# Ten instead of eight token blocks by Strassen products, with copies on ScalarE and the softmax division on GpSimd

## The chip, the cores and the metric

The kernel runs on one core of a Trainium2 chip. The metric is the device time of one execution in microseconds (us), taken as the median of three runs. Beside it there is one profiled execution, which leaves a trace of every instruction.

## The reference

There are 8 batches of 8 heads, 576 positions and head size 64. The attention keeps only the scores within tau of the row's maximum; its result, heads side by side, feeds a layer with an exact gelu (4608 tokens, 512 wide, 2048 hidden).

```python
scores = scale * np.matmul(q, k.transpose(0, 1, 3, 2))
thresh = np.max(scores, axis=-1, keepdims=True) - tau
scores = np.where(scores >= thresh, scores, -1000000000.0)
scores = scores - np.max(scores, axis=-1, keepdims=True)
attn = np.exp(scores)
attn = attn / (np.sum(attn, axis=-1, keepdims=True) + 1e-09)
x = (attn @ v), as (B, H, S, D) -> (B*S, H*D)
h = x @ w_in
g = 0.5 * h * (1.0 + erf(h / sqrt(2)))
out = g @ w_out
```

The two weight matrices come as 64-bit floats; the kernel makes 32-bit floats of them from their bits.

## The kernel before

**Work and its pieces.** Two heads make a pair, and there are 32 pairs, four to a batch. A pair's scores are made in chunks of 128 query rows: for each of the first four chunks both heads side by side, and in a fifth, small one the last 64 rows of both heads together. One such chunk step is a slot (`scores`, `softmax_head`, `softmax_tail`), so a pair has five slots, and a batch 20. In a slot TensorE writes scores into two PSUM tiles of two banks each (tag `sc`, two buffers; the fifth slot uses one); VectorE takes each row's negated maximum (L368); GpSimd makes the threshold from it (L369); ScalarE takes the exponential (L371); VectorE then compares the scores with the threshold and multiplies (L387, with a row sum), which frees the score tile for the next slot. VectorE turns the result in 32x32 blocks (L434, L432), and SyncE's DMAs put these together as pT (`regroup`, L456 and L452). Two slots into the next pair, TensorE multiplies v by pT (`weigh_v`, L473, in two parts of 320 and 256 tokens), and the result, x transposed, is divided by the row sums on its way from PSUM to the x tiles (L490, VectorE). The reciprocals travel through DRAM and come back on all partitions as inv (`divisors`, L409 to L422).

**The first batch is done in another way.** Its four pairs (the "early" ones, slots 0 to 19: first chunks 0 and 1 of all four pairs, then the rest of each) are transposed by TensorE with a diagonal matrix of reciprocals (`turn_p_early`, L302), copied from PSUM by ScalarE (L310, L320) and, for the last chunk, by VectorE (L313, L325). Meanwhile the weights are converted in 32 pieces: `conversions` takes exponents (L178, VectorE), rebases them (L179, ScalarE), takes mantissas (L185) and puts these together (L187, L189). This needs three tiles of the pool `gp` for each piece, which also holds the gelus' results.

**The MLP.** The 4608 tokens are 18 blocks of 256. Ten are plain: `block_steps` yields the products one by one, 64 of the first layer (hT, L530, 256 columns) and 32 of the second (o_ps, L543, 512 columns), and `fill` puts as many into each slot, behind its scores, as a written plan allows. On TensorE a product of 32-bit floats is two instructions in the trace. The plan is GOAL: so many blocks done by such a slot, with PARTS sharing a pair's amount among its five slots (1.2, 1.2, 0.8, 1.2, 0.6). Every engine takes its instructions in the order written. A gelu (L509) needs another table of ScalarE's than the exponentials do, so each row of gelus is followed by a tiny exponential that brings the other table back (`table`, L516): two table loads per row. From slot 20 on, the gelus that have come due are done after the next slot's exponentials; in the early slots on even slots only, and as they come.

**The last stage.** The other eight blocks are done two at a time after all attention (`strassen`, L663), by the seven products of quarters that Strassen's scheme, in Winograd's form, needs in place of eight. The tokens are one dimension of a quarter: the two blocks of a pair are its two halves. The x of blocks that wait for this stage stays in the pool `xg` (seven tiles), but three of them (AWAY: blocks 10 to 12) are written to DRAM as soon as they are ready (`put_away`, SyncE) and fetched back during the stage (`bring`).

**GpSimd** also issues the DMAs of later pairs' q, k and v (`load_steps`, one step a slot: q in slot 1, k in slot 2, v in slots 3 and 4, four DMAs each). Queries are multiplied by the scale on ScalarE (L338) in slot 2, between VectorE's transposes of k and q (L337, L339).

Of the kernel before, what the change touches and what calls it, by code (L numbers as in the profile page):

```python
# [8 lines left out]
FP32 = mybir.dt.float32  # L9
U32 = mybir.dt.uint32  # L10
U8 = mybir.dt.uint8
AF = mybir.ActivationFunctionType
# [6 lines left out]
def kernel(  # L19
# [33 lines left out]
    P = 128  # L53
# [11 lines left out]
    N_DF = d_ff // P  # L65
    TOK = 256
    N_BLK = B * S // TOK
    PLAIN = N_BLK - 8

    AWAY = [PLAIN, PLAIN + 1, PLAIN + 2]  # L70
    order = list(range(PLAIN + 3, N_BLK)) + AWAY
    DUOS = list(zip(order[0::2], order[1::2]))
    assert 2 * D == P and 2 * TAIL == P and HALF <= 512 and N_DM == HP and B * S % TOK == 0 and S % Q == 0 and TOK == 2 * P
    SLOTS = NC + 1
# [86 lines left out]
    def conversions():  # L161

        vec = nc.vector
        ahead = None  # L170
        while raws or ahead:
            piece = None
            if raws:
                dst, raw, shifted = raws.pop(0)
                hi = raw.rearrange("p (f w) -> p f w", w=2)[:, :, 1]
                top = shifted.rearrange("p (f w) -> p f w", w=2)[:, :, 0]
                expo, power = (gp.tile([P, PIECE], U32, tag="g", name=s) for s in ("expo", "power"))
                vec.tensor_scalar(expo, hi, 0x7FF00000, None, op0=ALU.bitwise_and)  # L178
                nc.scalar.activation(power, expo, AF.Relu, bias=rebias, scale=8.0)  # L179
                piece = dst, hi, top, power  # L180
                yield 340
            if ahead:
                dst, hi, top, power = ahead
                mant = gp.tile([P, PIECE], U32, tag="g", name="mant")
                vec.tensor_scalar(mant, top, 0x0FFFFFFF, 0x10000000, op0=ALU.bitwise_and, op1=ALU.bitwise_or)  # L185
                yield 340
                vec.scalar_tensor_tensor(power, hi, 0x80000000, power, op0=ALU.bitwise_and, op1=ALU.bitwise_or)  # L187
                yield 720
                vec.scalar_tensor_tensor(dst, mant, 2.0 ** -28, power.bitcast(FP32), op0=ALU.mult, op1=ALU.mult)  # L189
                load_piece()  # L190
                converted[0] += 1
                yield 700
            ahead = piece
# [98 lines left out]
    def turn_p_early(p, i):  # L292


        s = st[p]
        if i == 0 or (p < HP and i == 2):
            s["pT"] = [one.tile([P, KR, S], FP32, tag=f"pT{e}", name=f"pT{e}") for e in range(2)]
        w, diag = s.pop(("p", i)), s.pop(("diag", i))
        n = 1 if i == NC else 2

        def turn(to, cols, e):
            nc.tensor.matmul(to, lhsT=w[:, cols], rhs=diag[:, e, :], start=True, stop=True)  # L302

        for e in range(n):
            tr = ps.tile([P, NC, P], FP32, tag="mm", name="tr")
            for c in range(NC):
                at = e * (S + TAIL) + c * P
                turn(tr[:, c, :], slice(at, at + P), e)
            if i < NC:
                nc.scalar.copy(s["pT"][e][:, 0:NC, i * P:(i + 1) * P], tr)  # L310
        if i == NC:
            for e in range(2):
                nc.vector.tensor_copy(s["pT"][e][:, 0:NC, MAIN:S], tr[:, :, e * TAIL:(e + 1) * TAIL])  # L313
        tails = s["pT"][0][:, NC, :]
        tr = ps.tile([P, NC, P], FP32, tag="mm", name="tr")
        if i < NC:
            for e in range(2):
                at = MAIN + e * TAIL
                turn(tr[e * TAIL:(e + 1) * TAIL, 0, :], slice(at, at + TAIL), e)
            nc.scalar.copy(tails[:, i * P:(i + 1) * P], tr[:, 0, :])  # L320
            return
        turn(tr[0:TAIL, 0, :], slice(MAIN, S), 0)
        for e in range(2):
            rows = slice(e * TAIL, (e + 1) * TAIL)
            nc.vector.tensor_copy(tails[rows, MAIN:S], tr[0:TAIL, 0, rows])  # L325

    def turn_qk(p):

        s = st[p]
        qT = s["qT"] = ld.tile([P, MAIN], FP32, tag="qT", name="qT")
        kT = s["kT"] = ld.tile([P, S], FP32, tag="kT", name="kT")
        qt = s["q_tail"] = q_tail[p % 4]
        qs, ks = s.pop("q"), s.pop("k")
        nc.vector.transpose(kT.rearrange("p (b i) -> p b i", i=Q), ks)  # L337
        nc.scalar.activation(qs, qs, AF.Copy, bias=0.0, scale=q_scale)  # L338
        nc.vector.transpose(  # L339
            qT.rearrange("p (c a i) -> p c a i", c=NC, i=Q),  # L340
            qs[:, 0:MAIN // Q, :].rearrange("p (a c) j -> p c a j", c=NC))
        for e in range(2):
            rows = slice(e * D, (e + 1) * D)
            nc.vector.transpose(
                qt[rows, e * TAIL:(e + 1) * TAIL].rearrange("p (b i) -> p b i", i=Q), qs[rows, MAIN // Q:NB, :])
# [112 lines left out]
    def weigh_v(p, lo, hi):  # L458
# [5 lines left out]
        for c in range(KR):  # L464
            for e in range(2):
# [4 lines left out]
                else:  # L470
# [1 line left out]
                    rhs = by_64(s["pT"][e])[:, lo // (2 * Q):hi // (2 * Q), c, :]  # L472
                nc.tensor.matmul(  # L473
                    to, lhsT=s["v"][:, e, c, :], rhs=rhs, start=(c == 0), stop=(c == KR - 1))
        by = None if p < EARLY else s["inv"]
        if hi == S:
            del st[p]

        def divide():
            at = lo  # L480
            while at < hi:
                n, o = divmod(b * S + at, TOK)
                size = min(TOK - o, hi - at)
                if n not in x_blk:
                    x_blk[n] = xg.tile([P, N_DM, TOK], FP32, tag="x", name="x")
                to, x = x_blk[n][:, hp, o:o + size], xT[:, at - lo:at - lo + size]
                if by is None:
                    nc.scalar.copy(to, x)
                else:
                    nc.vector.tensor_tensor(to, x, by[:, at:at + size], op=ALU.mult)  # L490
                at += size

        if by is not None:
            return divide
        divide()


    NS_IN, NS_OUT = 4 * TOK / 2.4, 4 * d_model / 2.4
# [2 lines left out]
    late = []  # L501
    lag = [1]
    dirty = [False]
    def gelus(left):

        while len(late) > left:
            g, j, hT = late.pop(0)
            t = gp.tile([P, 2, TOK], FP32, tag="g", name="g")
            nc.scalar.activation(t, hT, AF.Gelu)  # L509
            g[j - 1], g[j] = t[:, 0, :], t[:, 1, :]  # L510
            dirty[0] = True

    def table():

# [4 lines left out]
    def block_steps(n):  # L519
# [15 lines left out]
        for m in range(TOK // P):  # L535
            for j in range(N_DF):
                mlp["layer"] = 2
                yield NS_OUT, len(pieces) - N_DF + j + 1
                if j not in g:
                    gelus(0)  # L540
                if j == 0:
                    o = ps.tile([P, 512], FP32, tag="mm", name="o_ps")
                nc.tensor.matmul(o[:, 0:d_model], lhsT=g[j][:, m * P:(m + 1) * P], rhs=w_out_sb[j],  # L543
                                 start=(j == 0), stop=(j == N_DF - 1))
# [237 lines left out]
    BATCH = HP * SLOTS  # L782
    WIDE = 5 * 2 * Q
    WEIGH = 2
    START = 2 * HP + 2

    GOAL = [(-1, 0.0), (START - 1, 0.0), (BATCH - 1, 0.55)]
    GOAL += [(BATCH * (m + 2) + WEIGH, x) for m, x in enumerate([1.96, 3.3, 4.64, 5.98, 7.32, 8.66, PLAIN])]

    def goal(n):  # L790
        for (lo, x), (hi, y) in zip(GOAL, GOAL[1:]):
# [7 lines left out]
    tokens = 0  # L799
    owed = 0.0  # L800
    due = []
    loads = iter(())
    for n in range(len(slots) + WEIGH + 1):
        p, i = slots[n] if n < len(slots) else divmod(n, SLOTS)
# [4 lines left out]
            softmax_head(p, i)  # L809
        elif n == len(slots):  # L810
            ext = weights_in()
        if not early or n % 2 == 0:
            gelus(0)
            table()
        made = []
        for args in due:
            weigh_v(*args)
        due = []
        if p > EARLY and i == WEIGH:
            made = [weigh_v(p - 1, lo, hi) for lo, hi in ((0, WIDE), (WIDE, S))]  # L820
        owed += (goal(n) - goal(n - 1)) * BLK_NS * (PARTS[i] if not early and p < NP else 1.0)
        if early:
            fill(owed, tokens)
# [3 lines left out]
            turn_p_early(*last)  # L827
        if p < NP:
            softmax_tail(p, i)
        if made:  # L830
            made[0]()
        if p < NP and not early:
            turn_p(p, i)
        if made:
            made[1]()
        if p < NP and not early:
            if i == 2:
                regroup(p, 1)
# [16 lines left out]
        if n == BATCH:  # L855
            for t in pd_tail + [turned_p[:, e, h, :, :] for e in range(2) for h in range(2)]:
                nc.gpsimd.memset(t[:, NB:4 * KR, :], 0.0)
        if p >= HP and i == 1 and p + 2 < NP:
            loads = load_steps(p + 2)
        if p >= HP:  # L860
            next(loads, None)
        if p >= HP - 1 and i == 2 and p + 1 < NP:
            turn_qk(p + 1)
        convert(3000 if n < 2 * HP else 3650 if n < BATCH - 1 else 1e9)
# [11 lines left out]
        if n == START - 1:  # L876
            tokens = TOK
        elif n == BATCH + 1:
            tokens = S
        elif p > EARLY and i == WEIGH and p % HP == 0:  # L880
            tokens = p // HP * S
            for n in AWAY:
                if n in x_blk and (n + 1) * TOK <= tokens:
                    put_away(n)
    fill(1e12, B * S)
    strassen(*ext)

# [31 lines left out]
```

## Time and profile before

| what | us |
|---|---|
| median of 3 runs (1420.29 to 1422.51) | 1420.45 |
| profiled execution, its own time | 1423.59 |
| its span in the trace | 1421.8 |
| TensorE matmuls busy | 1382.1 (97%) |
| VectorE busy | 892.6 (63%) |
| ScalarE busy | 640.9 (45%) |
| GpSimd busy | 388.0 (27%) |
| table loads on ScalarE, 71 ahead of gelus and 71 behind | 91.1 each |
| division on VectorE (L490), 104 instructions | 31.8 |
| first Strassen product starts | 1028.79 |

Three stages follow each other. To about 160 us the first batch and the weights are prepared; to about 1029 us come 28 pairs of attention, with plain blocks between their steps; then four passes of two blocks by Strassen. In the page's slices each digit is one fortieth of the span, 35.5 us, in tenths of busy time. In the chain and the timeline a line gives start, duration, engine, line and operation, and in brackets how long an engine was idle before, and on whom it waited.

### The profile page before, as it was taken

What the parts mean: (1) busy time and instruction counts of PE and PEld (TensorE: products, weight loads), DVE (VectorE), ACT (ScalarE), POOL (GpSimd) and SP (SyncE); (2) the same over time, 40 slices, a digit from 0 to 9 for tenths busy, and PEclk for the clock granted to TensorE, in tenths of its full rate; (3) what the DMA queues carried; (4) which work ended last, traced back from release to release, by engine and by line L of the source; (5) the groups of instructions that cost most, each with busy time, mean ns of one, the idle gap of its engine ahead of it and who ended that gap; (6) DMA issues with size and microseconds to landing.
All of it is one profiled execution on the core that took longest, in us unless ns stands there. A gap on an engine that the chain in (4) does not pass through costs nothing.

```text
span 1421.8 us, 19662 instructions
## 1 busy us (share of the span) xinstructions
PE 1382.1 (97%) x6544; PEld 958.8 (67%) x6544; DVE 892.6 (63%) x1788; ACT 640.9 (45%) x1040; POOL 388.0 (27%) x812
## 2 busy tenths in 40 slices
PE   6898999999999999999999999999999999999999
PEld 4666547566466574665756647566588888888887
DVE  5887777777777777777777777777764142241330
ACT  5758525436356273462645727547141140230320
POOL 4443244434433433434434434430000000000000
PEclk9999999999999999999999999999999999999999
DMA  9977167776666676666766666674500000001000
GB/s 265 295 264 243 38 145 150 148 156 129 134 136 148 146 156 129 146 135 149 162 148 146 158 146 150 141 160 101 106 3 8 23 1 26 19 1 48 12 8 23
DMA packets 219347, 167.05 MB, mean 117 GB/s; under 512 B 122480, under 2 KB 203952, under 8 KB 219248
## 3 DMA queue, kind: packets, MB, share of 16 engines
q1 hardware_dynamic: 193040, 108.65, 36.2%
q0 software_dynamic: 23808, 56.57, 13.1%
q8 instruction: 53, 0.87, 0.3%
q10 hardware_dynamic: 2400, 0.59, 0.2%
q14 instruction: 46, 0.38, 0.1%
HBM read 71.68 MB, written 11.47 MB: 58 GB/s over the span
## 4 chain that ended last, share of the span: by engine, by line
PE 87%; DVE 5%; ACT 5%; DMA 2%; issue 1%; SPq 0%; POOL 0%; DVEq 0%; ACTq 0%; POOLq 0%
PE bank L663 27%; PE o_ps L543 18%; PE hT L530 18%; PE sc L356 12%; PE xT L473 10%; ACT p L371 1%; DVE p L387 1%; PE tr L302 1%; DVE power L187 1%; DMA q<-in_q_dram 1%; DVE nmx L368 1%; ACT L509 1%; ACT diag L401 1%; DMA turned_p<-in_moe_w_in_dram 1%; ACT power L179 0%
## 5 line engine op out<-in xcount | busy, mean ns | idle before, releaser
L371 ACT ACTIVATE p<-sc,nmx 128x576 f32<-128x576 f32 x288 | 202.4, 739 | 383.9 <-DVE nmx L368 383.8
L368 DVE TENSOR_REDUCE nmx<-sc 128x1 f32<-128x576 f32 x288 | 205.0, 749 | 158.8 <-PE sc L356 158.7
L530 PE MATMUL hT<-x,w_in 128*128 128x256 f32 x1280 | 296.2, 384 | 0.0
L543 PE MATMUL o_ps<-w_out,g 128*128 128x512 f32 x640 | 295.1, 604 | 0.0
L530 PEld LDWEIGHTS hT<-x,w_in 128*128 128x128 f32 x1280 | 238.4, 190 | 56.4 <-issue 24.7
L387 DVE SCALAR_TENSOR_TENSOR p<-sc,thr,p 128x576 f32<-128x576 f32 x288 | 225.4, 816 | 65.2 <-ACT p L371 64.1
L369 POOL TENSOR_SCALAR thr<-nmx,tau_eff 128x1 f32<-128x1 f32 x288 | 84.3, 293 | 547.7 <-DVE nmx L368 547.6
L543 PEld LDWEIGHTS o_ps<-w_out,g 128*128 128x128 f32 x640 | 117.1, 190 | 140.0 <-issue 138.2
L356 PE MATMUL sc<-kT,qT 64*128 64x288 f32 x960 | 165.9, 435 | 2.8 <-DVE p L387 2.5
L473 PE MATMUL xT<-pT,v 128*64 128x256 f32 (+1 forms) x1280 | 163.7, 409 | 2.7 <-ACT g L509 2.7
L434 DVE STREAM_TRANSPOSE turned_p<-p 128x1152 f32<-128x1152 f32 x112 | 154.1, 1376 | 3.0
L356 PEld LDWEIGHTS sc<-kT,qT 64*128 64x128 f32 x960 | 93.7, 188 | 84.2 <-issue 71.8
L473 PEld LDWEIGHTS xT<-pT,v 128*64 128x64 f32 x1280 | 89.8, 137 | 74.1 <-issue 12.7
L234 POOL DMA_DIRECT2D v<-in_v_dram x208 | 110.5, 534 | 10.7 <-issue 9.8
L663 PE MATMUL bank<-x,w_in 128*128 128x256 f32 x384 | 93.3, 379 | 0.0
L663 PE MATMUL bank<-w_out,unit 128*128 128x256 f32 x416 | 92.4, 379 | 0.0
L516 ACT ACT_TABLE_LOAD x71 | 91.1, 1283 | 1.3
L509 ACT ACT_TABLE_LOAD x71 | 91.1, 1283 | 1.2
L663 PEld LDWEIGHTS bank<-w_out,unit 128*128 128x128 f32 x416 | 79.0, 190 | 10.7
L663 PEld LDWEIGHTS bank<-x,w_in 128*128 128x128 f32 x384 | 73.0, 190 | 10.3 <-issue 0.5
L225 POOL DMA_DIRECT2D q<-in_q_dram x104 | 70.7, 685 | 16.0 <-issue 15.1
L302 PE MATMUL tr<-diag,p 128*128 128x128 f32 (+1 forms) x360 | 51.4, 311 | 19.6 <-ACT diag L401 11.4
(148 smaller groups left out, 1326.8 us busy)
## 6 DMA issues: line engine op xcount, KB each, us to landing
pT<-turned_p SPq DMA_DIRECT2D x448, 160.0 KB, 3.6
pT<-pd_tail SPq DMA_DIRECT2D x112, 80.0 KB, 2.9
q<-in_q_dram POOLq DMA_DIRECT2D x104, 72.0 KB, 4.1
k<-in_k_dram POOLq DMA_DIRECT2D x104, 72.0 KB, 2.6
inv<-turned SPq DMA_DIRECT2D x56, 128.0 KB, 3.9
v<-in_v_dram POOLq DMA_DIRECT2D x156, 40.0 KB, 3.3
out_dram<-o_sb SPq DMA_DIRECT2D x20, 256.0 KB, 4.4
raw<-in_moe_w_in_dram POOLq DMA_DIRECT2D x8, 512.0 KB, 5.2
```

Of the source, the lines that this page charges most:

```text
L234: eng.dma_start(t[r:P:4, e, 0:n, :], rows[:, r * KR:r * KR + n, :])
L356: nc.tensor.matmul(sc[e][:, h, 0:HALF], lhsT=lhsT, rhs=s["kT"][rows, at:at + HALF], start=True, stop=True)
L368: nc.vector.tensor_reduce(nmx[:, e:e + 1], sc, axis=AXIS.XY, op=ALU.max, negate=True)
L371: nc.scalar.activation(w[:, e * S:(e + 1) * S].rearrange("p (h s) -> p h s", h=2), sc, AF.Exp, bias=nmx[:, e:e + 1], scale=1.0)
L387: nc.vector.scalar_tensor_tensor(row, sc[e][:, :, 0:HALF], thr[:, e:e + 1], row, op0=ALU.is_ge, op1=ALU.mult, accum_out=den[e])
L434: nc.vector.transpose(turned_p[:, :, i // 2, 0:NB, i % 2 * Q:(i % 2 + 1) * Q], w.rearrange("p (e b i) -> p e b i", e=2, i=Q))
L473: nc.tensor.matmul(to, lhsT=s["v"][:, e, c, :], rhs=rhs, start=(c == 0), stop=(c == KR - 1))
L509: nc.scalar.activation(t, hT, AF.Gelu)
L516: nc.scalar.activation(warm[:, 1:2], warm[:, 0:1], AF.Exp)
L530: nc.tensor.matmul(hT[:, j % 2, :], lhsT=w_in_sb[c][:, j * P:(j + 1) * P], rhs=x_blk[n][:, c, :], start=(c == 0), stop=(c == N_DM - 1))
L543: nc.tensor.matmul(o[:, 0:d_model], lhsT=g[j][:, m * P:(m + 1) * P], rhs=w_out_sb[j], start=(j == 0), stop=(j == N_DF - 1))
L663: nc.tensor.matmul(to, lhsT=l, rhs=r, start=start and k == 0, stop=k == len(pairs) - 1, skip_group_check=not start)
```

## The change

It consists of these parts:

- PLAIN falls from 10 to 8 blocks, so ten blocks go by Strassen, in five passes; blocks 8 to 12 are the ones that are put away. GOAL plans 0.5 blocks by the end of the early slots and about one block a batch afterwards, where it planned 0.55 and 1.34.
- `weigh_v` no longer divides: ScalarE copies x transposed from PSUM to the x tile. A slot later (DIVIDE = 3) GpSimd multiplies the pair's 576 columns in place by inv, in three instructions.
- In the last early chunk, ScalarE copies pT where VectorE did (L313, L325).
- Up to slot 20, ScalarE only copies hT from PSUM (`hold`); in slot 20 all these gelus are done in a row, in place, between two table loads. They are no longer held back on odd slots.
- Queries are scaled in slot 1 (`scale_q`), ahead of slot 2's exponentials.
- Blocks to be put away go one at a time, in slots 0 and 1 (`leaving`).
- The conversion uses one `gp` tile a piece: the exponents are rebased in place, and the mantissas go into the destination.

```diff
-    PLAIN = N_BLK - 8
-    AWAY = [PLAIN, PLAIN + 1, PLAIN + 2]
-    order = list(range(PLAIN + 3, N_BLK)) + AWAY
+    PLAIN = N_BLK - 10
+    AWAY = list(range(PLAIN, PLAIN + 5))
+    order = list(range(PLAIN + 5, N_BLK)) + AWAY
...
-                expo, power = (gp.tile([P, PIECE], U32, tag="g", name=s) for s in ("expo", "power"))
-                vec.tensor_scalar(expo, hi, 0x7FF00000, None, op0=ALU.bitwise_and)
-                nc.scalar.activation(power, expo, AF.Relu, bias=rebias, scale=8.0)
+                power = gp.tile([P, PIECE], U32, tag="g", name="power")
+                vec.tensor_scalar(power, hi, 0x7FF00000, None, op0=ALU.bitwise_and)
+                nc.scalar.activation(power, power, AF.Relu, bias=rebias, scale=8.0)
...
-                nc.vector.tensor_copy(s["pT"][e][:, 0:NC, MAIN:S], tr[:, :, e * TAIL:(e + 1) * TAIL])
+                nc.scalar.copy(s["pT"][e][:, 0:NC, MAIN:S], tr[:, :, e * TAIL:(e + 1) * TAIL])
...
-            nc.vector.tensor_copy(tails[rows, MAIN:S], tr[0:TAIL, 0, rows])
+            nc.scalar.copy(tails[rows, MAIN:S], tr[0:TAIL, 0, rows])
+
+    def scale_q(p):
+        t = st[p]["q"]
+        nc.scalar.activation(t, t, AF.Copy, bias=0.0, scale=q_scale)
...
-        nc.scalar.activation(qs, qs, AF.Copy, bias=0.0, scale=q_scale)
...
+        for n, o, at, size in in_blocks(b, lo, hi):
+            if n not in x_blk:
+                x_blk[n] = xg.tile([P, N_DM, TOK], FP32, tag="x", name="x")
+            nc.scalar.copy(x_blk[n][:, hp, o:o + size], xT[:, at - lo:at - lo + size])
...
+    def divide(p):
+        b, hp = divmod(p, HP)
+        by = st.pop(p)["inv"]
+        for n, o, at, size in in_blocks(b, 0, S):
+            x = x_blk[n][:, hp, o:o + size]
+            nc.gpsimd.tensor_tensor(x, x, by[:, at:at + size], op=ALU.mult)
...
-            nc.scalar.activation(t, hT, AF.Gelu)
-            g[j - 1], g[j] = t[:, 0, :], t[:, 1, :]
-            dirty[0] = True
+            if hold[0]:
+                nc.scalar.copy(t, hT)
+                held.append((g, j, t))
+            else:
+                gelu(g, j, t, hT)
...
+    def gelus_held():
+        hold[0] = False
+        while held:
+            g, j, t = held.pop(0)
+            gelu(g, j, t, t)
...
-    GOAL = [(-1, 0.0), (START - 1, 0.0), (BATCH - 1, 0.55)]
-    GOAL += [(BATCH * (m + 2) + WEIGH, x) for m, x in enumerate([1.96, 3.3, 4.64, 5.98, 7.32, 8.66, PLAIN])]
+    GOAL = [(-1, 0.0), (START - 1, 0.0), (BATCH - 1, 0.5)]
+    GOAL += [(BATCH * (m + 2) + DIVIDE, x) for m, x in enumerate([1.96, 2.97, 3.98, 4.98, 5.99, 6.99])]
+    GOAL += [(BATCH * B + WEIGH, PLAIN)]
...
-        if not early or n % 2 == 0:
-            gelus(0)
-            table()
+        gelus(0)
+        if n == BATCH:
+            gelus_held()
+        table()
...
+        if EARLY < p < NP and i == DIVIDE:
+            divide(p - 1)
...
+        if p >= HP and i == 1 and p + 1 < NP or p == HP - 1 and i == 2:
+            scale_q(p + 1)
...
-        elif p > EARLY and i == WEIGH and p % HP == 0:
+        elif p > EARLY and i == DIVIDE and p % HP == 0 or p == NP and i == WEIGH:
             tokens = p // HP * S
-            for n in AWAY:
-                if n in x_blk and (n + 1) * TOK <= tokens:
-                    put_away(n)
+            leaving += [n for n in AWAY if n in x_blk and (n + 1) * TOK <= tokens]
+        elif leaving and i < 2:
+            put_away(leaving.pop(0))
```

More of the change, by code (lines that the diff above doesn't have):

```diff
@@ L176, in conversions @@
                 top = shifted.rearrange("p (f w) -> p f w", w=2)[:, :, 0]
-                expo, power = (gp.tile([P, PIECE], U32, tag="g", name=s) for s in ("expo", "power"))
-                vec.tensor_scalar(expo, hi, 0x7FF00000, None, op0=ALU.bitwise_and)
-                nc.scalar.activation(power, expo, AF.Relu, bias=rebias, scale=8.0)
-                piece = dst, hi, top, power
+                power = gp.tile([P, PIECE], U32, tag="g", name="power")
+                vec.tensor_scalar(power, hi, 0x7FF00000, None, op0=ALU.bitwise_and)
+                nc.scalar.activation(power, power, AF.Relu, bias=rebias, scale=8.0)
+                piece = dst, hi, top, dst.bitcast(U32), power
                 yield 340
             if ahead:
-                dst, hi, top, power = ahead
-                mant = gp.tile([P, PIECE], U32, tag="g", name="mant")
+                dst, hi, top, mant, power = ahead
                 vec.tensor_scalar(mant, top, 0x0FFFFFFF, 0x10000000, op0=ALU.bitwise_and, op1=ALU.bitwise_or)
@@ L474, in weigh_v, with in_blocks @@
                     to, lhsT=s["v"][:, e, c, :], rhs=rhs, start=(c == 0), stop=(c == KR - 1))
[L475 to L495, printed above, removed]
+        for n, o, at, size in in_blocks(b, lo, hi):
+            if n not in x_blk:
+                x_blk[n] = xg.tile([P, N_DM, TOK], FP32, tag="x", name="x")
+            nc.scalar.copy(x_blk[n][:, hp, o:o + size], xT[:, at - lo:at - lo + size])
+    def in_blocks(b, lo, hi):
+        while lo < hi:
+            n, o = divmod(b * S + lo, TOK)
+            size = min(TOK - o, hi - lo)
+            yield n, o, lo, size
+            lo += size
+    def divide(p):
[4 more added lines that the diff above has]
+            nc.gpsimd.tensor_tensor(x, x, by[:, at:at + size], op=ALU.mult)
     NS_IN, NS_OUT = 4 * TOK / 2.4, 4 * d_model / 2.4
@@ L503 @@
     dirty = [False]
+    held = []
+    hold = [True]
     def gelus(left):
@@ L508, in gelus, with gelu @@
             t = gp.tile([P, 2, TOK], FP32, tag="g", name="g")
-            nc.scalar.activation(t, hT, AF.Gelu)
-            g[j - 1], g[j] = t[:, 0, :], t[:, 1, :]
-            dirty[0] = True
+            if hold[0]:
[3 more added lines that the diff above has]
+                gelu(g, j, t, hT)
+    def gelu(g, j, t, src):
+        nc.scalar.activation(t, src, AF.Gelu)
+        g[j - 1], g[j] = t[:, 0, :], t[:, 1, :]
+        dirty[0] = True
+    def gelus_held():
[3 more added lines that the diff above has]
+            gelu(g, j, t, t)
     def table():
@@ L784 @@
     WEIGH = 2
+    DIVIDE = 3
     START = 2 * HP + 2
-    GOAL = [(-1, 0.0), (START - 1, 0.0), (BATCH - 1, 0.55)]
-    GOAL += [(BATCH * (m + 2) + WEIGH, x) for m, x in enumerate([1.96, 3.3, 4.64, 5.98, 7.32, 8.66, PLAIN])]
+    GOAL = [(-1, 0.0), (START - 1, 0.0), (BATCH - 1, 0.5)]
+    GOAL += [(BATCH * (m + 2) + DIVIDE, x) for m, x in enumerate([1.96, 2.97, 3.98, 4.98, 5.99, 6.99])]
+    GOAL += [(BATCH * B + WEIGH, PLAIN)]
     def goal(n):
@@ L801 @@
     due = []
+    leaving = []
     loads = iter(())
@@ L811 @@
             ext = weights_in()
-        if not early or n % 2 == 0:
-            gelus(0)
-            table()
-        made = []
+        gelus(0)
+        if n == BATCH:
+            gelus_held()
+        table()
         for args in due:
@@ L819 @@
         if p > EARLY and i == WEIGH:
-            made = [weigh_v(p - 1, lo, hi) for lo, hi in ((0, WIDE), (WIDE, S))]
+            for lo, hi in (0, WIDE), (WIDE, S):
+                weigh_v(p - 1, lo, hi)
+            if p == NP:
+                divide(p - 1)
         owed += (goal(n) - goal(n - 1)) * BLK_NS * (PARTS[i] if not early and p < NP else 1.0)
@@ L829 @@
             softmax_tail(p, i)
-        if made:
-            made[0]()
         if p < NP and not early:
             turn_p(p, i)
-        if made:
-            made[1]()
         if p < NP and not early:
@@ L857 @@
                 nc.gpsimd.memset(t[:, NB:4 * KR, :], 0.0)
+        if EARLY < p < NP and i == DIVIDE:
+            divide(p - 1)
         if p >= HP and i == 1 and p + 2 < NP:
```

## The prediction

> **What bounds the kernel now.** I read the page's slices first, then TensorE's waits, the chain of waits over the last third, and the timeline of one head pair. The slices:
>
> ```profile
> PE   6898999999999999999999999999999999999999
> DVE  5887777777777777777777777777764142241330
> ACT  5758525436356273462645727547141140230320
> ```
>
> TensorE is full from about 200 us on; only the first six slices have holes. From 205 us to the end TensorE waits 6.4 us in all, by its waits. So a block moved from one method to the other is worth its TensorE time, if the other engines keep up. The chain gives that time without overlap, first over one head pair of attention (five slots, each with its scores), then over one pass of the last stage:
>
> ```profile
> 951.90 1.69 PE sc L356 x8
> 953.60 4.51 PE hT L530 x20
> 958.11 1.17 PE sc L356 x8
> 959.28 4.51 PE hT L530 x20
> 963.80 1.17 PE sc L356 x8
> 964.97 5.00 PE xT L473 x40
> 969.97 3.22 PE hT L530 x14
> 973.19 1.17 PE sc L356 x8
> 974.36 4.95 PE hT L530 x22
> 979.30 0.97 PE sc L356 x4
> 980.27 2.16 PE hT L530 x10
> 982.43 1.70 PE sc L356 x8
> ...
> 1076.79 96.97 PE bank L663 x448
> 1173.76 0.02 issue
> 1173.79 0.43 DVE turned_p L713
> 1174.22 0.04 issue
> ```
>
> The pair takes 30.53 us: scores 5.65, weighing 5.00, plain blocks (hT) 19.35, and 0.53 of wait inside the first scores of the next pair (1.70 instead of 1.17). A Strassen pass takes 97.5 us for two blocks (1076.79 to 1174.26). The timeline shows what sets that 0.53, and the room of the other engines, where a one-chunk slot follows a two-chunk slot (columns: start, duration, engine, line):
>
> ```profile
> 612.33 0.08 DVE L387 DVE_READ_ACCUMULATOR p<-sc,thr,p 128x1 f32 x1
> 612.33 0.81 DVE L387 SCALAR_TENSOR_TENSOR p<-sc,thr,p 128x576 f32<-128x576 f32 x1
> ...
> 616.38 0.29 POOL L369 TENSOR_SCALAR thr<-nmx,tau_eff 128x1 f32<-128x1 f32 x1 [2.27 <-DVE nmx L368]
> ```
>
> The scores of that two-chunk slot end at 609.84; VectorE frees their second bank at 613.14, 3.3 us later, and TensorE takes it about 0.12 later. With some 4.5 us of plain work behind its scores TensorE never notices. After the one-chunk slot (scores end 615.24, thresholding ends 617.9) the next scores need until 3.94 us after the previous ones: 2.25 us of plain work and 1.17 of scores leave the 0.52 of wait.
>
> **The Trainium skill.** "GPSIMD Engine Reference", section 3.1, measures a two-input fp32 operation of 2048 columns at 4497 ns on GpSimd, 2.2 ns a column; the trace before has no such GpSimd row, so it can't confirm this. "SBUF — State Buffer", section "Who interferes with whom", has GpSimd and VectorE exclude each other where VectorE reads two SBUF inputs; VectorE's thresholding here reads one from PSUM, so I charge nothing. "ScalarE: Activation LUTs", section "What ACT_TABLE_LOAD costs", gives 1283 ns a load; the trace agrees (1283, x71 on each of two lines).
>
> **The change part by part**, against the profiled execution: span 1421.8, own time 1423.6, 3.1 above the median of 1420.45. I carry the difference over to the median.
>
> *Two blocks change method.* A plain block is 128 hT instructions at 4.51/20 = 0.2255 us and 64 of o_ps at 0.449 (4.49 for 10 elsewhere in the chain): 28.9 + 28.7 = 57.6. Two fewer: -115.2. One more pass: +97.5. Sum -17.7. Its sums on VectorE and its two blocks fetched back lie beside TensorE, as in the four passes now, which join with 0.5 us between them.
>
> *The cover that goes.* Plain work covers the softmax chain. The built program's order of instructions gives it slot by slot for the 25 whole pairs after the first: a two-chunk slot mostly gets 8 products of hT (3.61 us) or 4 of o_ps (3.60) where it got 10 or 5 (4.5); the one-chunk slot gets 1.80 in 24 of 25. The need is 3.3 + 0.12 = 3.41 in the first, 3.94 - 1.17 = 2.77 in the second. So the one-chunk slot waits 0.97: 24 x 0.97 + 0.5 = 23.8, against 12.1 before (4 at 0.97, 15 at 0.52, 6 at 0.07). Of the two-chunk slots, 12 get only 3.15 (wait 0.26) and 6 get 2.7 (wait 0.71): 7.4, against nothing. Together +19.1. This takes the gain.
>
> *VectorE loses the division* (L490, 104 instructions, 31.8 us) and eight small pT copies; it is not what is late in a slot with weighing (TensorE needs 8.4 there), so this gains nothing in the stage. *ScalarE gets the copies:* some 3.5 a pair at about 0.29, 1.0 us, in the weighing slot, behind its exponentials and a gelu (6.5 us after the scores), so done by 7.8, before the next scores at 8.4: nothing. The query scaling (0.76) moves one slot up and makes the weighing slot's exponentials 0.8 late: covered there. A slot with a gelu costs ScalarE 1.41 + 1.28 + 0.60 + 1.28 + 0.20 = 4.8 us with gaps, as long as the new slot (3.61 + 1.17 = 4.78): I charge 0.2 for each of 12 pairs with gelus in a row, +2; 0 to 8.
>
> *GpSimd gets three multiplications a pair*, 576 columns. They stand behind the thresholds of the fourth slot and ahead of a V load (2.14) and the one threshold of the one-chunk slot. GpSimd sits idle 2.27 before that threshold; the slot gets 0.8 shorter; thresholding follows 0.4 after it. So up to about 1.9 us is free; beyond that each us delays the one-chunk slot of every pair. Price: 576 x 2.2 ns = 1.25, and a fixed part of 0.09 (the 128x640 memset, 625 ns at 0.83 a column) to 0.29 (a threshold) each: 1.5 to 2.1. I take 1.8 and charge +1; the ends are 0 and +7.
>
> *SyncE:* put_away goes from three to five blocks, each now up to 3 slots later and behind the divisors' transfers. Those on p must land before the second half of the weighing, which comes some 29 us after the first (26.5 + 2.6); now they land 25 to 27.5 after it and start no later, so 1.5 to 4 us are left: nothing. The last pair has little filler behind it; its weighing comes about 4 us sooner and meets that landing: +1.5.
>
> *The first stage.* Between 84 and 165 us TensorE waits for ScalarE (view of waits):
>
> ```profile
> PE tr L302 <- ACT g L509: 5.0, 4, 2.3
> PE tr L302 <- ACT pT L310: 2.4, 3, 0.8
> ```
>
> With 0.7 on x this is 8.1 us. Seven gelus there bring 14 table loads, 18.0 us; plain copies of the same length need none. I take 6.5 of the 8.1 back, 2.2 for the granted clock (0.86 to 0.91 in three of these 15 us stretches, which follow the holes), and 1.0 for 1.2 us of copies off VectorE where scores wait for it: -9.7. Against it, slot 20: behind exponentials that end at 167.44 come a copy, a load and the first gelu, so the second layer starts at 169.9 where TensorE is free at 167.4: 2.5. The other gelus hold the last pT copies until 176.8, where the weighing is ready at 175.6: 1.2. With 1.3 for the clock after the hole: +5. Net -4.7; -10 to +2. The conversion's in-place tiles change no operation: nothing.
>
> *Sum:* -17.7 + 19.1 + 2 + 1 + 1.5 - 4.7 = +1.2: 1424.8 for the profiled execution, 1421.7 at the median. 0.2% (2.8 us) is about what a measurement here can tell from no change.
>
> **Rivals.** *A, forecast:* the lost cover eats the gain; 1421.7, own range 1417 to 1427. *B, slower:* GpSimd's division is late for the one-chunk slot's threshold. It decides from 1.9 us a pair; for it speaks the other GpSimd row, 600 ns for a 128x2 addition: 1.25 + 3 x 0.4 = 2.45, 0.55 late x 28 pairs = +15, 1437. Against it the 293 ns of the other row. *C, faster:* the first stage gives its whole 10 us and the row of gelus hides behind TensorE's own work: -6.5, and no ScalarE lateness, -2: 1413. For it the 18 us of loads; against it that TensorE is already 90% busy there. *D, slower:* ScalarE becomes the bound in slots with gelus, 4.8 against 4.78, and lateness adds up over neighbouring slots: +8, 1430.
>
> **How the numbers follow.** A 0.42, B 0.20, C 0.24, D 0.14. A's own range leaves 0.03 below 1417.6 and 0.06 above 1423.3. Faster 0.24 + 0.03 = 0.27; slower 0.20 + 0.14 + 0.06 = 0.40; same 0.33. The range reaches to C and B: 1412 to 1437.
>
> **What would show it.** Right: the chain shows 57.6 us a block and 97.5 a pass unchanged, five passes, a head pair of about 26.5 us, and in the pair's first scores 2.1 us instead of 1.7, with TensorE waiting for thresholding some 30 us in all. B right: thresholding waits for thr on GpSimd, and the division rows sum to over 1.9 a pair. C right: the first Strassen pass starts over 102 us sooner than at 1028.8. A is wrong if TensorE's waits on thresholding stay under 20 us, or if it waits for transfers in the weighing.

## The result, and the profile after

| | before | after |
|---|---|---|
| median of 4 runs (lowest to highest), us | 1420.41 (1420.29 to 1422.51) | 1422.41 (1421.36 to 1423.81) |
| profiled execution, its own time, us | 1423.59 | 1421.36 |
| its span, us | 1421.8 | 1419.5 |
| TensorE's first instruction behind the scores of slot 20, us from the span's start | 165.87 | 150.09 |
| the same of slot 30 | 224.77 | 214.74 |
| the same of slot 158, the last pair's fourth | 1005.19 | 907.85 |
| first Strassen product starts | 1028.79 | 929.04 |

The ratio of after to before is 1.0011, interval 0.9994 to 1.0029: no difference that can be measured. The profiled execution of before was slower than its four runs and that of after is the fastest of its four, so the traces differ by -2.3 us where the medians differ by +2.0; the sums below compare the traces. Slot 158's scores come 97.3 us sooner, where 115.2 us of plain work have gone; the fifth pass takes 97.5 back.

The slices of the page after, for TensorE and VectorE, look as full as before; from them alone the loss can't be seen:

```profile
PE   6899999999999999999999999999999999999999
DVE  5988577778888878877877887765033142241330
```

The chain of waits shows it. First a head pair of after, from its first scores to the next pair's; then a pass (start, duration, engine, line):

```profile
861.11 1.21 PE sc L358 x6
862.31 4.08 PE hT L546 x18
866.39 1.17 PE sc L358 x8
867.56 3.65 PE hT L546 x16
871.21 1.17 PE sc L358 x8
872.38 5.00 PE xT L475 x40
877.39 2.36 PE hT L546 x10
879.74 1.22 PE sc L358 x8
880.96 0.75 DVE nmx L370
...
884.18 1.38 DVE turned_p L436
885.55 0.00 issue
885.56 0.77 DVE nmx L370
...
888.16 1.21 PE sc L358 x6
```

```profile
977.03 96.98 PE bank L680 x448
```

Before, the chain stayed on TensorE for the whole pair. Now it leaves TensorE behind the fourth slot's scores (880.96) and goes through maximum, exponential and thresholding of two slots until the next pair's scores (888.16): in these 7.2 us TensorE does its scores and plain products too, but the softmax sets the time. The pair takes 27.05 us where it took 30.53; a pass takes 97.5 as before (977.03 to 1074.51).

The one-chunk slot of another pair, with GpSimd's new work (in brackets what an engine waited for):

```profile
587.91 1.70 POOL L494 TENSOR_TENSOR x<-x,inv 128x256 f32<-128x256 f32 x3
589.55 2.15 POOL L233 DMA_DIRECT2D v<-in_v_dram  x4
591.74 0.31 POOL L371 TENSOR_SCALAR thr<-nmx,tau_eff 128x1 f32<-128x1 f32 x1
592.38 0.82 DVE L389 SCALAR_TENSOR_TENSOR p<-sc,thr,p 128x576 f32<-128x576 f32 x1 [0.88 <-ACT p L373]
```

GpSimd reaches the threshold without idle time, where it had stood idle 2.27 before; but thresholding still waits for the exponential, not for it. The view of waits of TensorE from 200 to 1000 us names the loss, and understates it:

```profile
PE sc L358 <- DVE p L389: 11.3, 25, 0.9
```

Eleven us, 25 times. The view counts only the time after the modelled end of the matmul before. If one takes how long each slot's scores last beyond their bare 1.17 us (0.97 in a one-chunk slot), slots 30 to 158 lose 33.0 us, 29.7 of them in the pair's first scores; before, 13.7. Sums of waits below are made in this second way.

In slot 20, the row of gelus:

```profile
154.61 7.18 PE L560 MATMUL o_ps<-w_out,g 128*128 128x512 f32 x10 [3.00 <-ACT g L519]
```

Ten instructions of the second layer wait 3.0 us and then take 7.18 us instead of 4.5: the granted clock is 0.79 from 150 to 166 us.

### The profile page after: what moved, and what is told of

Same layout as the page of the kernel before. It is cut to its first block, busy times and chain, and to the rows that moved or that the text cites. A ratio compares the mean times of both kernels' runs of the same rounds, so it can differ in the third digit from the quotient of the medians.

```text
span 1419.5 us, 19992 instructions
## 1 busy us (share of the span) xinstructions
PE 1375.2 (97%) x6608; PEld 970.4 (68%) x6608; DVE 888.3 (63%) x1734; ACT 636.8 (45%) x1164; POOL 433.9 (31%) x896
## 4 chain that ended last, share of the span: by engine, by line
PE 80%; DVE 10%; ACT 7%; issue 1%; DMA 1%; SPq 1%; ACTq 0%; DVEq 0%
PE bank L680 34%; PE hT L546 12%; PE o_ps L560 11%; PE sc L358 11%; PE xT L475 10%; DVE p L389 4%; ACT p L373 3%; DVE nmx L370 2%; PE tr L301 2%; DVE turned_p L436 1%; ACT L519 1%; ACT L532 1%; DVE power L186 1%; DVE w_in L188 1%; DMA q<-in_q_dram 0%
## 5 line engine op out<-in xcount | busy, mean ns | idle before, releaser
L389 DVE SCALAR_TENSOR_TENSOR p<-sc,thr,p 128x576 f32<-128x576 f32 x288 | 225.5, 816 | 74.3 <-ACT p L373 72.3
L370 DVE TENSOR_REDUCE nmx<-sc 128x1 f32<-128x576 f32 x288 | 204.0, 745 | 97.3 <-PE sc L358 97.0
L560 PE MATMUL o_ps<-w_out,g 128*128 128x512 f32 x512 | 241.1, 610 | 3.0 <-ACT g L519 3.0
L546 PE MATMUL hT<-x,w_in 128*128 128x256 f32 x1024 | 241.1, 385 | 0.0
L546 PEld LDWEIGHTS hT<-x,w_in 128*128 128x128 f32 x1024 | 189.6, 190 | 50.1 <-issue 25.3
L560 PEld LDWEIGHTS o_ps<-w_out,g 128*128 128x128 f32 x512 | 93.5, 192 | 113.8 <-issue 108.6
L680 PE MATMUL bank<-x,w_in 128*128 128x256 f32 x480 | 116.7, 379 | 0.0
L680 PE MATMUL bank<-w_out,unit 128*128 128x256 f32 x520 | 115.5, 379 | 0.0
L680 PEld LDWEIGHTS bank<-w_out,unit 128*128 128x128 f32 x520 | 98.8, 190 | 13.4
L680 PEld LDWEIGHTS bank<-x,w_in 128*128 128x128 f32 x480 | 91.2, 190 | 12.8 <-issue 0.5
L680 PE MATMUL bank<-v,unit 128*128 128x256 f32 x320 | 82.1, 379 | 0.0
L680 PE MATMUL bank<-unit,turned_p 128*128 128x256 f32 x320 | 73.1, 379 | 0.0
```

The costliest lines, as they stand in the source:

```text
L370: nc.vector.tensor_reduce(nmx[:, e:e + 1], sc, axis=AXIS.XY, op=ALU.max, negate=True)
L389: nc.vector.scalar_tensor_tensor(row, sc[e][:, :, 0:HALF], thr[:, e:e + 1], row, op0=ALU.is_ge, op1=ALU.mult, accum_out=den[e])
L546: nc.tensor.matmul(hT[:, j % 2, :], lhsT=w_in_sb[c][:, j * P:(j + 1) * P], rhs=x_blk[n][:, c, :], start=(c == 0), stop=(c == N_DM - 1))
L680: nc.tensor.matmul(to, lhsT=l, rhs=r, start=start and k == 0, stop=k == len(pairs) - 1, skip_group_check=not start)
```

## The experiments

The theory on trial is A, that the softmax chain, with less plain work in the pair to cover it, takes the gain. (Cover is the plain work behind a slot's scores, which keeps TensorE busy until the softmax chain has freed the score tiles.) Times are medians; the kernel before has its own median in each set, 1421.78 in the first, 1423.35 in the second, 1422.29 in the third.

**Cover given back (parts).** No work changes; only where the plain products stand.

```diff
-    PARTS = 1.2, 1.2, 0.8, 1.2, 0.6
+    PARTS = 1.24, 1.24, 0.32, 1.26, 0.94
```

> The changed kernel, with the plain work of a head pair shared among its five slots as 1.24, 1.24, 0.32, 1.26, 0.94 instead of 1.2, 1.2, 0.8, 1.2, 0.6: work is taken from the slot with the weighing and given to the one-chunk slot. Counted from the built order of instructions, the waits for thresholding should fall from 32 us to about 2. Theory A (the cover taken from the softmax chain ate the gain): 22 to 30 us faster than the changed kernel, 1393 to 1401. Rival (VectorE, ScalarE or GpSimd is as late as TensorE there, so that cover alone isn't what is short): within 5 us of the changed kernel, 1417 to 1427, the waits reappearing in the slot with the weighing.

Measured 1394.28, ratio to before 0.9805 (0.9789 to 0.982): some 28 us below the changed kernel. The chain of a pair is TensorE's alone again, and the next pair's first scores last 1.28:

```profile
461.45 5.00 PE xT L475 x40
466.45 1.06 PE o_ps L560 x2
467.51 1.17 PE sc L358 x8
468.68 3.63 PE o_ps L560 x8
472.31 0.97 PE sc L358 x4
473.28 2.57 PE o_ps L560 x6
475.85 1.28 PE sc L358 x8
```

The waits in slots 30 to 158 fall from 33.0 to 3.6 us, and that stretch from 693.1 to 663.7 us. A holds. It also shows that the 33 us weren't the price of the new method: the slot with the weighing had cover to spare.

**The other edits alone (plan10).** Ten plain blocks again.

```diff
-    PLAIN = N_BLK - 10
+    PLAIN = N_BLK - 8
-    AWAY = list(range(PLAIN, PLAIN + 5))
+    AWAY = list(range(PLAIN, PLAIN + 3))
...
-    GOAL += [(BATCH * (m + 2) + DIVIDE, x) for m, x in enumerate([1.96, 2.97, 3.98, 4.98, 5.99, 6.99])]
+    GOAL += [(BATCH * (m + 2) + DIVIDE, x) for m, x in enumerate([1.96, 3.3, 4.64, 5.98, 7.32, 8.66])]
```

(The order of the blocks in the last stage follows AWAY.)

> The changed kernel with ten plain blocks and eight by Strassen again, as before the change (three blocks put away, about 1.34 blocks planned a batch); every other part of the change stays. Theory A (those other parts cost nothing in the pairs, and the gelus in a row give a net 6 to 7 us early): 1413 to 1416. Rival D or B (copies on ScalarE or the division on GpSimd cost time in the pairs, which the early gain hides): 1420 or more.

Measured 1416.13, ratio 0.9955 (0.9941 to 0.9969), at the upper edge of what A foresaw. From slot 30 to 158 it takes 781.25 us, against 780.42 before, with 2.2 us more plain work there: in pairs with cover, the copies on ScalarE, the division on GpSimd and the earlier query scaling cost nothing. The gain is the first stage's: TensorE is through with slot 30's scores at 212.39 us, before at 224.77.

**The same with shares that cover (plan10p).**

```diff
-    PARTS = 1.2, 1.2, 0.8, 1.2, 0.6
+    PARTS = 1.2, 1.2, 0.55, 1.2, 0.85
```

> The kernel with ten plain blocks again and every other edit of the change (1416.1 measured), with a pair's plain work shared as 1.2, 1.2, 0.55, 1.2, 0.85, so that its one-chunk slots too have enough of it. Counted from the built order, waits for thresholding fall from 11 to 0.5 us: 1404 to 1408. Theory A then says what two blocks more by Strassen are worth when both plans have their cover: this minus the kernel with eight plain blocks and moved shares (1394.3) should be 9 to 17 us, toward the 17.7 of TensorE's own work. Rival (the shares alone make the difference, and the blocks bring nothing): within 5 us of 1394.3.

Measured 1405.87, ratio 0.9882 (0.9865 to 0.9898); waits 0.9 us. Against the ratio of parts, 0.9805, two blocks more by Strassen are worth 0.0077, 11 us, once both plans have their cover. TensorE's work alone says 17.7; in the traces the spans differ by 12.7, 2.7 of the rest being the waits that parts has more. So the gain is real. In the changed kernel the loss was larger than it: from plan10 to that kernel, with the same shares, the ratio rises from 0.9955 to 1.0011, some 8 us, while the waits go from 12.0 to 33.0. The two blocks alone, with the shares as they stood, make the kernel slower; that the change as a whole came out even is owed to the first stage.

**The division on VectorE again (divvec, divlate).** In the first it stands where it stood before the change, one part ahead of the transpose of p and one behind it; in the second behind the transposes of the next pair's k and q, at the end of the same slot.

```diff
-            nc.scalar.copy(x_blk[n][:, hp, o:o + size], xT[:, at - lo:at - lo + size])
+            nc.vector.tensor_tensor(to, x, st[p]["inv"][:, at:at + size], op=ALU.mult)
...
-            nc.gpsimd.tensor_tensor(x, x, by[:, at:at + size], op=ALU.mult)
```

(`to` and `x` are the two operands of the removed copy. In the first batch the copies stay. The lines that move the call are left out.)

> The changed kernel with the division back on VectorE, on the way from PSUM to the x tile, as before the change; no copies by ScalarE of the pairs after the first batch and no multiplication on GpSimd. Theory A: thresholding waits for GpSimd 1.7 us in all in the changed kernel, and VectorE has room in the slot with the weighing, so 1420 to 1424, as the changed kernel. Rival B (the division on GpSimd makes thresholds late): 5 to 15 us faster, 1407 to 1417. If VectorE has no room: slower, 1426 or more.

Measured 1437.97, ratio 1.0108 (1.0093 to 1.0124): some 15 us above the changed kernel, in the direction of the third case, but not for its reason. VectorE in the slot with the weighing:

```profile
399.53 0.55 DVE L486 TENSOR_TENSOR x<-xT,inv 128x128 f32<-128x128 f32 x2 [3.35 <-DMA inv<-turned]
400.00 1.37 DVE L436 STREAM_TRANSPOSE turned_p<-p 128x1152 f32<-128x1152 f32 x1
401.29 0.45 DVE L486 TENSOR_TENSOR x<-xT,inv 128x64 f32<-128x64 f32 x2
...
403.42 1.42 DVE L370 TENSOR_REDUCE nmx<-sc 128x1 f32<-128x576 f32 x2
```

It stands idle for 3.35 us until the reciprocals land; everything behind it, down to the maximum of scores that were ready at about 401, is late, and TensorE then stands 1.36 us ahead of the one-chunk slot's scores (406.03). The view of waits has VectorE waiting for reciprocals 17 times, 32.7 us; TensorE's waits on thresholding are 24.3 us in it, against 11.3 in the changed kernel. Before the change VectorE never waited so: pairs of 30.5 us leave the round trip through DRAM time enough, pairs of 27 us don't.

> The changed kernel with the division on VectorE from PSUM, as in the run that took 1438.0, but placed at the end of the slot with the weighing, behind the transposes of the next pair's k and q, instead of ahead of the transpose of p and behind it. No work is taken away. If what cost there was VectorE standing still for the reciprocals on their way through DRAM (17 waits, 32.7 us): those waits fall under 8 us and the time to 1420 to 1428. If what cost was VectorE's own time for the division (0.3 us each, 104 of them): 1434 to 1440, as before.

Measured 1422.64, ratio 0.9999 (0.9988 to 1.0009), with 1.0 us of waits for reciprocals in all, and the same 32.8 us of waits in the scores as the changed kernel. So the 104 divisions take no more time on VectorE in a free place than on GpSimd, where they cost nothing that plan10 could tell; what costs is a place ahead of the transfer that they need.

**More work on GpSimd (pool1, pool2).** One or two instructions behind each division; the reciprocals that they square aren't read again.

```diff
+        again = by[:, 0:TOK]
+        nc.gpsimd.tensor_tensor(again, again, again, op=ALU.mult)
```

> The changed kernel with one GpSimd instruction more behind each pair's division: 256 columns of the reciprocals, which nobody reads any more, times themselves; 0.73 us by the rows of the trace, so GpSimd's work there goes from 1.70 to 2.43 us a pair. Rival B's rule of the prediction (free up to 1.9 us a pair, every us beyond delays the one-chunk slot's threshold): 0.53 us late in some 27 pairs, 14 us more than the changed kernel, 1434 to 1439. If GpSimd has 2.5 us of room or more: 1421 to 1425.

> The same with two such instructions, 3.16 us a pair. By the rule 1.26 us late in some 27 pairs, 34 us more than the changed kernel, 1452 to 1460; 20 us above the kernel with one, whatever the point from which it decides, if that is below 2.4. If the lateness is hidden by other work: within 5 us of the kernel with one.

Measured 1428.15, ratio 1.0036 (1.0023 to 1.0049), and 1450.66, ratio 1.0204 (1.0187 to 1.0221). VectorE's waits on GpSimd, in the first, then in the second (us in all, times, longest); in the changed kernel they are 1.7, 4 times:

```profile
DVE p L389 <- POOL thr L371: 30.3, 33, 1.3
```

```profile
DVE p L389 <- POOL thr L371: 45.7, 28, 2.0
```

The time of pool1 falls between the two cases foreseen, that of pool2 just under its range. The two lines overstate the loss, for VectorE's waits on the exponential fell meanwhile from 72.3 us to 47.5 and 45.4: both kinds together rise by 3.8 us, then by 13.3 more.

The instruction took 0.61 us, not 0.73. From slot 30 to 158 the kernels (the changed one, pool1, pool2) take 693.1, 698.1 and 718.4 us: +5.0 for the first 0.61, +20.3 for the second. The waits in the scores rise from 33.0 to 38.0 and to 53.8: over some 27 pairs 0.18 a pair for the first instruction and 0.59 for the second, nearly all of its length. The other 4.5 us don't show as waits. In pool2's profile, and in neither of the others, the granted clock is 0.50 in three stretches of 3.4 us of this stage (from 603.7, 743.6 and 856.3 us); by estimate that is up to 5 us. So rival B's mechanism is there. By an estimate from these figures (1.70 + 0.61 - 0.18) it decides at about 2.1 us a pair, not at 1.9, and the changed kernel stands 0.4 below.

**The early gelus as they come (nohold).**

```diff
-    hold = [True]
+    hold = [False]
```

> The changed kernel with the early gelus done as they come, each row between two table loads, instead of in one row in slot 20; everything else stays. From the traces, the row of gelus gave 12.6 us before slot 20 and took back about 6 behind it: if that reading holds, 1428 to 1430, that is 6 to 7 above the changed kernel, with TensorE waiting some 8 us for gelus and copies of ScalarE before slot 20. Rival (the early gain is another's, of the tiles of the conversion or of the copies on ScalarE): within 2 us of the changed kernel, 1421 to 1424.

Measured 1427.81, ratio 1.0043 (1.0028 to 1.0058), 5.4 above the changed kernel, just under what was expected. TensorE waits 8.2 us for ScalarE from 84 to 165 us, and it is through with slot 20's scores at 160.24, 10.2 later than in the changed kernel; by slot 30 only 4.5 of that is left. So the row of gelus gives 10.2 us, and takes 5.7 back in slot 20.

**Both lessons used (best).** The shares of parts; the row of gelus ahead of slot 20's exponentials, with ten products planned there; even shares in the first pair without a weighing.

```diff
-    GOAL = [(-1, 0.0), (START - 1, 0.0), (BATCH - 1, 0.5)]
-    GOAL += [(BATCH * (m + 2) + DIVIDE, x) for m, x in enumerate([1.96, 2.97, 3.98, 4.98, 5.99, 6.99])]
+    GOAL = [(-1, 0.0), (START - 1, 0.0), (BATCH - 1, 0.5), (BATCH, 0.63)]
+    GOAL += [(BATCH * (m + 2) + DIVIDE, x) for m, x in enumerate([1.87, 2.9, 3.92, 4.94, 5.96, 6.98])]
-    PARTS = 1.2, 1.2, 0.8, 1.2, 0.6
+    PARTS = 1.25, 1.25, 0.30, 1.26, 0.94
+    FIRST = 1.1, 1.1, 1.1, 1.1, 0.6
...
             scores(p, i)
+            if n == BATCH:
+                gelus(0)
+                gelus_held()
+                table()
             softmax_head(p, i)
```

(The call of `gelus_held` behind the exponentials goes, and FIRST stands for PARTS in that pair.)

> The changed kernel with three edits: the shares of a pair 1.25, 1.25, 0.30, 1.26, 0.94; the held gelus in slot 20 ahead of that slot's exponentials instead of behind them, with ten products of the second layer planned there instead of five; and even shares in the first pair after the early ones, which has no weighing (1.1 for four slots, 0.6 for the last), with the goals slightly flatter. Against the kernel with moved shares alone (1394.3): five products more in slot 20 in the same time (4.5 us), and the hole of 2.3 us in slot 22 filled; 1386 to 1390. Rival (the exponentials behind the gelus make slot 21's scores late, and take it back): 1393 to 1397.

Measured 1386.67 (1386.23 to 1387.73), ratio 0.9744 (0.9728 to 0.9759): 36 us faster than the kernel before. Slot 20's second layer:

```profile
154.44 8.85 PE L560 MATMUL o_ps<-w_out,g 128*128 128x512 f32 x20 [0.89 <-ACT g L519]
```

Twenty instructions in 8.85 us at full clock, behind a wait of 0.9 instead of 3.0; the exponentials behind the gelus make nobody late: from 150 to 214 us TensorE's waits on thresholding are 1.4 us, 1.6 in parts. The three edits were run together, so what each of them gave beyond parts is not shown.

## Why the prediction was right, and which terms were off

The time forecast was 1421.7 and the median is 1422.4, for the reason of A: a gain on TensorE and a loss of cover of about the same size. The terms, from the two traces; plain work is counted from the built order at 0.451 us a product of hT and 0.90 of o_ps:

| term | forecast | measured |
|---|---|---|
| two plain blocks less | -115.2 | -115.3 (3.1 before slot 30, 108.6 to slot 158, 3.6 after) |
| one pass more | +97.5 | +97.45 |
| lost cover, ScalarE's and GpSimd's lateness (19.1 + 2 + 1) | +22.1 | +21.3 (108.6 - 87.3) |
| last weighing | +1.5 | +1.2 (3.6 - 2.4) |
| first stage, slot 20 with it | -4.7 | -6.9 (3.1 - 10.0) |
| sum | +1.2 | -2.2 |

The trace ended 3.4 us below the sum; the medians, which the forecast carried it over to, 0.7 above. Neither is more than single runs of the kernel before differ (1420.2 to 1425.6), so the agreement within 1 us is luck: the first stage gave 2.2 us more than its term, and the traces and the medians moved in opposite directions. The balance of gain and loss is not. The pair shown takes 27.05 us, not the 26.5 named among the signs; by an estimate from the sum's own terms it would be about 27.1.

- **The cover.** The total is right, and so are its parts. Losses are counted beyond the bare 1.17 us. For want of cover in the one-chunk slot the next pair's first scores lose 0.96 us in 25 pairs and 0.53 in one, 24.5 in all (forecast 23.8, for 25 pairs). The short two-chunk slots were charged 7.4 us, and 3.3 of it shows in the next scores. The rest shows later: nine of the short slots are fourth ones, and there the next pair's first scores last 2.44 us (3.15 us of plain work behind the fourth slot's scores) or 2.77 (2.7 us), 3.8 us in all beyond the 0.96. That makes 7.1. In one of them:

```profile
830.07 1.38 DVE L436 STREAM_TRANSPOSE turned_p<-p 128x1152 f32<-128x1152 f32 x1
832.12 0.74 ACT L373 ACTIVATE p<-sc,nmx 128x576 f32<-128x576 f32 x1 [2.62 <-DVE nmx L370]
```

ScalarE had stood idle for 2.62 us; VectorE, busy with the fourth slot until 831.4, was late with the maximum. Lateness of ScalarE, rival D's mechanism, was charged 2 us. It is there in eight pairs, where a gelu with its two table loads makes the one-chunk slot's exponentials 0.14 to 0.28 us late (859.31 in the timeline), and comes to about 1.2: four pairs last 2.22 instead of 2.13, four 2.65 instead of 2.44. It costs where cover is missing: in parts only two pairs' first scores last over 1.4 us. Some 2 us of the 21.3 I can't place, for the waits themselves rose by 19.3.

- **"A is wrong if TensorE's waits on thresholding stay under 20 us."** By the view of waits they do, at 11.3 us, and still A holds, as parts showed. The test was badly put: the 30 us had been counted from starts of instructions, and the view counts idle time behind modelled ends.
- **GpSimd.** Three multiplications take 1.70 us, forecast 1.8. Rows of 727 ns for 256 columns and 456 for 128 make 2.12 ns a column and some 0.18 us fixed; the Trainium skill's "GPSIMD Engine Reference", section 3.1, whose 2.2 a column priced it, is near. The charge of 1 us was too much, and so was B's chance: its fixed part of 0.4 came from an addition of two columns at 600 ns; the same addition of one column takes 610 in the trace before, so that time is another operation's and says little of a multiplication. Thresholding on VectorE, beside these multiplications, takes 816 ns on average in both traces, so to charge nothing there was right.
- **VectorE.** "This gains nothing in the stage" is right of the pairs as they were. What the prediction did not see is that pairs made shorter need the division to leave its old place: some 15 us, in divvec. A forecast part by part against the old pair misses such a pairing of edits.
- **The first stage.** Of -6.9, the row of gelus is -4.5 by nohold: 10.2 given (forecast 8.7) and 5.7 back (forecast 5). The remaining 2.4 are other edits there, charged 1.0, and not taken apart. C's mark, the first Strassen product over 102 us sooner, was missed at 99.75. It put this stage at 6.5 us beyond the forecast, -11.2, which is farther off than the -4.7; its other half, no lateness of ScalarE, was nearly so, with 1.2 us.
- **SyncE and the last pair.** No weighing before the last pair's waits for a transfer. In the last, TensorE stands 0.41 us in the middle, at 923.51, and the view names no transfer as the cause; the other 0.8 of the 1.2 us in the table are not placed.

## What to carry to other kernels

When work is moved off the bounding engine, ask what the moved instructions had been covering: the gain shows only where the chain behind them is shorter than what stays. Count the cover slot by slot from the built order against the latency that each kind of slot needs, and share what is left by need; that was worth 28 us here, with no work changed. And when a stage gets shorter, look at every transfer that had just had time enough.

## What the runs showed of the hardware

The same wait of 3.0 us in slot 20 was followed by ten instructions in 7.1 to 7.5 us in five of the profiles (after, parts, divvec, divlate, pool1) and in 4.56 in three (plan10, plan10p, pool2). In after the granted clock is 0.50 from 153.1 to 159.9 us, and in the 3.41 us ahead of that TensorE was busy for 1.75. The Trainium skill's "TensorE: Matmul & The Clock Gate", Part 1, has the clock halved after an idle window of about 3.4 us that runs freely, so that the moment matters. The runs agree in that a gap of this length does it at some times and not at others. They differ in that this gap is shorter than the window, and TensorE worked for half of the stretch ahead of the change: the window need not be idle throughout. A wait of 0.9 us cost no clock (best).
